# One plan for the order of every engine's work, and y of a block in two halves of its tokens: attention with two feed-forward layers on one core

## The chip, the cores and the metric

One core of one Trainium2 chip runs the kernel. The metric is the device time of an execution in microseconds (us). Names of engines: PE is TensorE (matmuls), DVE is VectorE, ACT is ScalarE, POOL is GpSimd, SP is SyncE, whose queue issues nearly all DMAs.

## What is computed

```python
def reference(q, k, v, moe_w_in, moe_w_out, moe2_w_in, moe2_w_out):
    scores = q @ k.T / sqrt(64)                   # 4 batches, 8 heads, 576 tokens, 64 wide
    scores = where(0 <= rel < 128, scores - slope[h] * abs(rel), -1e9)
    x = (softmax(scores) @ v)                     # 2304 tokens x 512
    h = x @ moe_w_in                              # 512 -> 2048
    x = where(h > 0, h, exp(min(h, 0)) - 1) @ moe_w_out      # ELU, 2048 -> 512
    h = x @ moe2_w_in
    return (h * sigmoid(h)) @ moe2_w_out          # SiLU
```

The four weights come as 64-bit numbers, and the kernel makes 32-bit ones of them on the chip.

## The kernel before

**Precision.** Every large product is made of three matmuls: each operand is split into an upper half (a copy by ACT to the matmul's number type) and a lower half (what is left, a subtraction on DVE), and upper x upper, upper x lower and lower x upper are summed in PSUM. So each operand costs ACT and DVE an instruction before PE can use it. Names end in `h` and `l` for the halves.

**Weights.** A piece of weights is loaded into one of four `wraw` tiles (`load_w`, four early ones into a part of `acc`), rescaled on POOL and ACT (`rescale`, L146 and L148), joined to 32 bits on DVE (`sign` L153, `join` L158) and split (`halves`, L166 and L167). Weights of the first matrix are taken in pairs: `first`, `second` and `third` in `parts` form the sums for the seven products below (L200 to L206). The early eight weights have their lower halves made on POOL.

**Attention** runs in 36 units (a pair of 128-token groups by a pair of heads). A unit's scores (L501), the masking and row minimum on DVE (L509), the exponential on ACT (L514), the division on POOL (L560), the turn of the scores on PE (L540) with copies on DVE (L548) and ACT (L550), and the product with the values (L579, one for two units) are recorded by a hand-written loop, one unit per pass. In its gaps (`point`, `pop`) stand pieces of layer 1 for the first four of its 2048/128 = 16 slices of width, block by block of 512 tokens: `hidden` (h, L326) and `output` (y, L362). The fifth block comes after attention, together with 16 pieces of the fourth that are held back (`RESERVE`).

**The other slices** run in 15 steps, called k0 to k14 here: layer 1 in two sweeps of six slices over three blocks of 768 tokens (k0 to k2, k3 to k5), layer 2 in sweeps of six, six and four slices (k6 to k8, k9 to k11, k12 to k14). In a step, each pair of slices is one `quad`: seven products (L901) of the weights' sums with seven sums of x (the operands, made by `make` on ACT and DVE, or reloaded by `reload` from DRAM; `make_far` makes those of k6 early and stores them through the tile `xo`) instead of eight. Copies of partial results (`snap`, tiles `hs` and `h`, ACT L908), sums (`add`, DVE L912) and activations (L860 to L881) follow each, and what they give is split in `gh` and `gl`. Then y: eight or six groups of matmuls (L998), each added to `acc` on DVE (L1012). The last two pieces of y (six matmuls each) are put between the first products of the next step (`pend`, L1110). The seven tiles of the second matrix's weights (`w1h`, `w1l`) come free when y of the last block of a sweep is done.

**What sets the order.** The program is written down engine by engine in the order of the calls. Behind each product or piece of y stands `between`, which has an allowance in us: it runs the next stage of the activation chains (`chain`), then operations from `urgent` (the operands) and from `weight_op` as far as the allowance lasts. During attention, `weight_step` does so in fixed units (`WSLOTS`). Each engine runs its own list strictly in this order. Tiles come from rings of buffers.

Of the kernel before, what the change touches and what calls it, by code (L numbers as in the profile page):

```python
# [26 lines left out]
class Ring:  # L27


    def __init__(self, pool, n):  # L30
        self.slots = [pool] * n

    def add(self, pool, n):
        self.slots = [pool] * n + self.slots

    def next(self):
        pool = self.slots.pop(0)
        self.slots.append(pool)
        return pool
# [3 lines left out]
def attention_elu_silu_kernel(  # L43
# [21 lines left out]
    NFF = DFF // P  # L65
    scale = 1.0 / float(D) ** 0.5
    blocks = [(0, 2)] + [(g, 4) for g in range(2, NG, 4)]
    FIRST = {b * S // P for b in range(B) if b * S % P == 0}
    MID = {b * S // P: b * S % P for b in range(B) if b * S % P}
    AFTER = {g + 1: r for g, r in MID.items()}  # L70

    NB = len(blocks)
# [6 lines left out]

# [3 lines left out]
    NPRE = 2  # L83
    PAIRS = 3
    OUTS = 7
    OPEN = 5
    LAG = 7
    RESERVE = 16
    ORDER = ((0, 1, 2), (2, 1, 0)), ((2, 1, 0), (0, 1, 2), (2, 1, 0))
    WSLOTS = [*range(15), *range(24, 36)]  # L90
    PIECES = (1, 1, 2)
    BANKS = 3
    UNITS = [(t, hp) for t in range(NG // 2) for hp in range(NPAIR)]
    home = {}
    for bi, (g0, n) in enumerate(blocks):
        for g in range(g0, g0 + n):
            home[g] = bi, (g - g0) * P

    left = lambda name, bufs, **kw: ctx.enter_context(tc.tile_pool(name=name, bufs=bufs, side="left", **kw))
    acc_p = left("acc", 1)  # L100
    wraw_p = left("wraw", NRAW)
    dram_p = ctx.enter_context(tc.tile_pool(name="dram", bufs=1, space=bass.MemoryType.DRAM))
    early = ExitStack()
    e_p = early.enter_context(tc.tile_pool(name="e0", bufs=1, side="right"))
    g_p = early.enter_context(tc.tile_pool(name="g0", bufs=FIRST_F, side="right"))
    w_p = early.enter_context(tc.tile_pool(name="w0", bufs=FIRST_F, side="right"))
    x_p = early.enter_context(tc.tile_pool(name="x0", bufs=1, side="right"))
    banks = Ring(ctx.enter_context(tc.tile_pool(name="ps_m", bufs=BANKS, space=PSUM)), BANKS)

    def bank(name):  # L110
        return banks.next().tile([P, 4 * P], F32, tag="m", name=name)
# [3 lines left out]
    xt = {}  # L115

    ws = [(w1_in, w1_out), (w2_in, w2_out)]
    weights = {}
    owed = []
    raws = {}  # L120

    def load_w(kind, layer, f):
        w = ws[layer][kind]
        i = tasks.index((kind, layer, f))
        if i in SCRATCH:

            bi, i = SCRATCH[i]
            t = acc[bi][:, i * 2 * NKC * P:(i + 1) * 2 * NKC * P]
            t = t.bitcast(U32).rearrange("p (f w) -> p f w", w=2)
        else:  # L130
            t = wraw_p.tile([P, NKC * P, 2], U32, tag="wraw", name="wraw")
        if kind == 0:
            nc.sync.dma_start(
                t.rearrange("p (c f) w -> p c (f w)", c=NKC),
                w[:, f * 2 * P:(f + 1) * 2 * P].rearrange("(c p) f -> p c f", p=P))
        else:
            nc.sync.dma_start(t.rearrange("p f w -> p (f w)"), w[f * P:(f + 1) * P, :])
        raws[kind, layer, f] = t

    def rescale(kind, layer, f):  # L140

        t = raws[kind, layer, f]
        low, top = t[:, :, 0], t[:, :, 1]


        nc.gpsimd.tensor_scalar(f32(top), f32(top), 2.0 ** -112, 1.0, op0=ALU.mult, op1=ALU.mult)  # L146

        nc.scalar.activation(low.bitcast(I32), low, AF.Copy, scale=7.49 * 2.0 ** -32)  # L148

    def sign(kind, layer, f):  # L150
        t = raws[kind, layer, f]
        low, top = t[:, :, 0], t[:, :, 1]
        nc.vector.scalar_tensor_tensor(low, top, 0x80000000, low, op0=ALU.bitwise_and, op1=ALU.bitwise_or)  # L153

    def join(kind, layer, f):
        t = raws[kind, layer, f]
        low, top = t[:, :, 0], t[:, :, 1]
        nc.vector.scalar_tensor_tensor(top, top, 3, low, op0=ALU.logical_shift_left, op1=ALU.bitwise_or)  # L158

    def halves(pool, tag, src, w):  # L160

        h = pool.tile([P, w], F32R, tag=f"{tag}h", name=f"{tag}h")
        lo = pool.tile([P, w], F32R, tag=f"{tag}l", name=f"{tag}l")

        def lower(eng=nc.vector):
            eng.tensor_tensor(lo, f32(src), f32(h), op=ALU.subtract)  # L166
        return (h, lo), lambda: nc.scalar.activation(h, f32(src), AF.Copy), lower  # L167

    def parts(kind, layer, f):

        full = NKC * P
        w = full // 2
        if kind == 1 or (layer == 0 and f < FIRST_F):
            top = raws.pop((kind, layer, f))[:, :, 1]
            early_one = layer == 0 and f < FIRST_F
            pair, upper, lower = halves(w_p if early_one else out_p[0], f"w{kind}", top, full)

            def done():
                lower(nc.gpsimd if early_one else nc.vector)
                weights[kind, layer, f] = pair  # L180
            return [(0.0, upper), (0.7, done)]
        if f % 2 == 0:
# [3 lines left out]
            def done():  # L186
                lower()
                weights[kind, layer, f] = pair
# [28 lines left out]
    def part(kind, layer, f):  # L217
        for _, fn in parts(kind, layer, f):
            fn()
# [934 lines left out]
```

## Time and profile before

| | |
|---|---|
| time, median of 3 runs | 962.9 us (961.23 to 963.43) |
| the profiled execution: time, span | 966.37 us, 964.6 us |
| PE busy | 888.9 us (92%) |
| DVE, ACT, POOL busy | 608.0, 500.1, 134.3 us |
| mean granted TensorE clock | 0.966 of full |

The span is the time from the first to the last instruction. An engine is busy while one of its instructions runs; time in which it waits is idle, and the trace names the instruction that ended the wait. PE is busy nearly all the time, so its idle time and its slow stretches are what can be read as loss.

### The profile page before, as it was taken

How to read it: one execution, taken by the hardware profiler on the slowest of the kernel's cores; microseconds unless marked ns; L12 is line 12 of the kernel's file. 1: busy time of each engine (PE TensorE's matmuls, PEld its weight loads, DVE VectorE, ACT ScalarE, POOL GpSimd, SP SyncE). 2: the span in 40 equal slices, each digit the busy share in tenths (PEclk: the TensorE clock that was granted, in tenths of full speed). 3: DMA queues.
4: the chain of work that ended last, by engine and by line, in shares of the span. 5: the costliest groups of instructions: out<-in, count | busy, mean ns of one | idle time of the engine just before them, and what ended most of it. 6: DMA issues, size and time to landing. Idle time of an engine off the chain costs nothing. (4 is left out here: it accounts for less than half of the span.)

```text
span 964.6 us, 15023 instructions
## 1 busy us (share of the span) xinstructions
PE 888.9 (92%) x5520; PEld 786.2 (82%) x5520; DVE 608.0 (63%) x1375; ACT 500.1 (52%) x1191; POOL 134.3 (14%) x248
## 2 busy tenths in 40 slices
PE   6788998988788999988999798999998999999998
PEld 4666775666688999988999797798888898889997
DVE  6866658647687877887666766664566442564343
ACT  6666676645473646465444546564656151534321
POOL 7753332321110000111000011000011000000000
PEclk9789999989899999999999899999999999999999
DMA  9224263314712610246072832515136332116541
GB/s 315 91 84 141 78 215 112 96 50 180 280 48 97 241 34 1 88 163 241 3 304 87 318 128 89 220 31 229 44 109 218 120 128 102 43 46 229 203 157 66
DMA packets 55929, 131.00 MB, mean 136 GB/s; under 512 B 3760, under 2 KB 35760, under 8 KB 55856
## 3 DMA queue, kind: packets, MB, share of 16 engines
q1 hardware_dynamic: 55712, 129.91, 37.7%
q8 instruction: 44, 0.72, 0.3%
q14 instruction: 29, 0.24, 0.1%
q10 hardware_dynamic: 144, 0.13, 0.0%
HBM read 93.06 MB, written 36.96 MB: 135 GB/s over the span
## 5 line engine op out<-in xcount | busy, mean ns | idle before, releaser
L881 DVE TENSOR_TENSOR gl<-e,gh 128x384 fp32r<-128x384 f32 x168 | 94.2, 565 | 81.0 <-ACT gh L861 76.0
L146 POOL TENSOR_SCALAR wraw<-wraw 128x512 f32<-128x512 f32 x60 | 44.1, 736 | 574.4 <-DMA wraw<-in_moe_w_in_dram 277.2
L998 PE MATMUL y<-w1l,gh 128*128 128x512 f32 (+1 forms) x292 | 113.6, 389 | 0.5 <-DVE w1l L166 0.5
L998 PE MATMUL y<-w1h,gh 128*128 128x512 f32 (+1 forms) x292 | 113.6, 389 | 0.4 <-ACT w1h L167 0.4
L998 PE MATMUL y<-w1h,gl 128*128 128x512 f32 (+1 forms) x292 | 113.6, 389 | 0.0
L998 PE MATMUL y<-gh,w1h 128*128 128x384 f32 x288 | 97.7, 339 | 4.7 <-ACT w1h L167 4.7
L998 PE MATMUL y<-gl,w1h 128*128 128x384 f32 x288 | 97.6, 339 | 0.8 <-DVE gl L881 0.8
L998 PE MATMUL y<-gh,w1l 128*128 128x384 f32 x288 | 97.8, 340 | 0.3
L1012 DVE TENSOR_TENSOR acc<-y,acc 128x384 f32<-128x384 f32 (+2 forms) x85 | 51.4, 607 | 72.4 <-PE y L998 72.4
L514 ACT ACTIVATE p<-p,neg 128x192 f32<-128x192 f32 (+1 forms) x144 | 62.9, 439 | 30.0 <-DVE neg L509 30.0
L560 POOL TENSOR_SCALAR p<-p,sm 128x192 f32<-128x192 f32 (+1 forms) x144 | 62.0, 449 | 107.0 <-DVE sm L518 86.2
L998 PEld LDWEIGHTS y<-w1h,gl 128*128 128x128 f32 x292 | 55.3, 189 | 11.3
L908 ACT ACTIVATE hs<-b 128x384 f32<-128x384 f32 x42 | 20.2, 481 | 85.3 <-PE b L901 85.3
L998 PEld LDWEIGHTS y<-w1h,gh 128*128 128x128 f32 x292 | 55.2, 189 | 10.4 <-ACT w1h L167 0.8
L998 PEld LDWEIGHTS y<-w1l,gh 128*128 128x128 f32 x292 | 55.2, 189 | 10.3 <-DVE w1l L166 0.8
L998 PEld LDWEIGHTS y<-gh,w1h 128*128 128x128 f32 x288 | 54.9, 190 | 5.4 <-ACT w1h L167 5.4
L998 PEld LDWEIGHTS y<-gh,w1l 128*128 128x128 f32 x288 | 54.9, 191 | 1.3 <-DVE w1l L166 1.3
L998 PEld LDWEIGHTS y<-gl,w1h 128*128 128x128 f32 x288 | 54.8, 190 | 1.2 <-DVE gl L881 1.2
L901 PE MATMUL b<-t,wbh 128*128 128x384 f32 x168 | 44.8, 347 | 11.6 <-DVE hs L912 11.6
L540 PEld LDWEIGHTS pt<-ident,p 64*128 64x128 f32 x544 | 23.8, 152 | 37.2 <-POOL p L560 27.3
L901 PE MATMUL b<-t,wch 128*128 128x384 f32 x168 | 45.3, 351 | 9.5 <-ACT hs L908 9.5
L877 ACT ACTIVATE gh<-e 128x384 fp32r<-128x384 f32 x72 | 36.8, 524 | 32.7 <-DVE e L312 18.7
(157 smaller groups left out, 2183.0 us busy)
## 6 DMA issues: line engine op xcount, KB each, us to landing
t<-d SPq DMA_DIRECT2D x28, 768.0 KB, 6.3
wraw<-in_moe_w_in_dram SPq DMA_DIRECT2D x32, 512.0 KB, 5.5
b<-d SPq DMA_DIRECT2D x21, 768.0 KB, 6.0
wraw<-in_moe_w_out_dram SPq DMA_DIRECT2D x28, 512.0 KB, 3.8
d<-t SPq DMA_DIRECT2D x16, 768.0 KB, 7.3
d<-b SPq DMA_DIRECT2D x12, 768.0 KB, 3.8
k<-in_k_dram SPq DMA_DIRECT2D x16, 384.0 KB, 5.5
d<-xo SPq DMA_DIRECT2D x7, 768.0 KB, 3.6
```

Of the source, the lines that this page charges most:

```text
L146: nc.gpsimd.tensor_scalar(f32(top), f32(top), 2.0 ** -112, 1.0, op0=ALU.mult, op1=ALU.mult)
L514: nc.scalar.activation(dst, dst, AF.Exp, bias=m, scale=-1.0, accum_out=a)
L540: nc.tensor.transpose(ps[:, x, j, i, :], pt[half, j, e, c - x * PAD:c - x * PAD + P], ident[half, half])
L560: nc.gpsimd.tensor_scalar(dst, dst, by, 1.0, op0=ALU.mult, op1=ALU.mult)
L877: nc.scalar.activation(gh[:, s], tiles["e"], AF.Copy)
L881: nc.vector.tensor_tensor(gl[:, s], tiles["e"], f32(gh[:, s]), op=ALU.subtract)
L901: nc.tensor.matmul(t[name][:, 0:HALF], a[:, cs], x[:, j, c, :], start=(start and c == 0 and n == 0), stop=(c == 1 and n == 2), skip_group_ ...
L908: nc.scalar.activation(t[name], t[src][:, 0:HALF], AF.Copy)
L998: nc.tensor.matmul(t["ps"][:, 0:w], l, r, start=(f == 0 and x == 0), stop=(f == n - 1 and x == 2))
L1012: nc.vector.tensor_tensor(dst, t["ps"][:, 0:w], dst, op=ALU.add)
```

## The change

The order of the calls no longer sets the order on the engines. Every operation is first added to a plan, with its engine, an assumed duration, what it reads and writes and, for PE, a due time; from these the latest useful start of every other operation follows, back along its users. Then a list scheduler plays the whole kernel: whenever an engine is free, it takes the ready operation with the earliest latest start and writes it down. `Ring`, `between`, `weight_op`, `weight_step`, `WSLOTS`, `point`, `pop`, `RESERVE` and the allowances are gone; tiles are fixed, with dependences by key.

```diff
+class Plan:
+    LINK = 0.2
+    DMA_START = 1.8
+    DMA_RATE = 220.0e3
...
+    def run(self):
+        for op in reversed(self.ops):
+            op.late = min([op.due] + [b.late - self.LINK - op.cost - op.tail for b in op.before])
...
+                for eng in queues:
+                    if eng and free.get(eng, 0.0) > now:
+                        continue
+                    can = [x for x in queues[eng] if max(x[0], x[1].floor) <= now]
...
+                    x = min(can, key=lambda x: (x[1].late, x[1].n))
...
+                    if op.moved:
+                        port = max(port, now + self.DMA_START) + op.moved / self.DMA_RATE
+                        end = port
```

An operation is added like this; the early lower halves of the weights, and the two `gl` of the last early block, go to DVE:

```diff
-            def done():
-                lower(nc.gpsimd if early_one else nc.vector)
+        if layer == 0 and f < FIRST_F:
+            tag = ("w0", kind, f)
+            split_weight(tag, None, top, None, 4 * P, top_k, "DVE")
...
-            eng = nc.gpsimd if bi == NB - 1 and f < 2 else nc.vector
-            eng.tensor_tensor(gl[:, 0:w], tiles["e"][:, 0:w], f32(gh[:, 0:w]), op=ALU.subtract)
+        add("DVE", 0.15 + w / 950.0, lambda: nc.vector.tensor_tensor(T[gk[1]][:, 0:w], T[ek][:, 0:w], f32(T[gk[0]][:, 0:w]),
+                                                                 op=ALU.subtract), r=[ek, gk[0]], w=[gk[1]])
```

The units of attention are due every 5.2 us, and the pieces of a block are due evenly from the time its x is expected to that of the next block's. Three tiles hold turned scores instead of two. The activations' tiles `e` are three instead of four. The tiles `gh` and `gl` now hold a half of a block's tokens; y is done by halves, and the second half is merged into the first nine products of the next step:

```diff
-            first, rest = pieces[:OPEN], pieces[OPEN:]
-            return ([p for g in first for p in g[:-1]] + [g[-1] for g in first] + [p for g in rest for p in g])
+        return [[g for h, g in groups if h == half] for half in range(2)]
...
+    def merge(a, b):
+        if not b:
+            return list(a)
+        out = []
+        for i, x in enumerate(a):
+            out.append(x)
+            lo, hi = i * len(b) // len(a), (i + 1) * len(b) // len(a)
+            out += b[lo:hi]
+        return out
...
-            pend = ys[-2:] if k + 1 < len(steps) else []
-            for fn in ys[:len(ys) - len(pend)]:
+            for fn in merge(order[:SPAN], owed) + order[SPAN:]:
                 fn()
-                between(1.04 if layer == 0 else 1.36)
...
+            first, second_half = outputs(k)
+            first = open_first(first)
+            second_half = [p for g in second_half for p in g]
+            first = first[:2] + over[:1] + first[2:3] + over[1:] + first[3:]
+            if k + 1 < len(steps) and SPAN:
+                owed = second_half
```

The number of instructions on PE, ACT and SP and of DMAs is the same. What stands where:

On POOL in the first units (L560 and L492 are the scaling of a unit's scores `p`; L166 is a weight's lower half; L146 and L315 rescale a weight), before:

```order
L483 COPY biasa<-bias 128x1536
L484 MEMSET biasa 64x8x64
L166 TENSOR_TENSOR w0l<-wraw,w0h 128x512
L146 TENSOR_SCALAR wraw<-wraw 128x512
L560 TENSOR_SCALAR p_120<-p_120,sm 128x128
L560 TENSOR_SCALAR p_120<-p_120,sm 128x192
L560 TENSOR_SCALAR p_120<-p_120,sm 128x128
L560 TENSOR_SCALAR p_120<-p_120,sm 128x192
L166 TENSOR_TENSOR w0l<-wraw,w0h 128x512
L146 TENSOR_SCALAR wraw<-wraw 128x512
```

and now:

```order
L436 MEMSET biasa 64x8x64
L492 TENSOR_SCALAR p_127<-p_127,sm_151 128x128
L492 TENSOR_SCALAR p_127<-p_127,sm_151 128x192
L492 TENSOR_SCALAR p_127<-p_127,sm_151 128x128
L492 TENSOR_SCALAR p_127<-p_127,sm_151 128x192
L315 TENSOR_SCALAR raw_85<-raw_85 128x512
L315 TENSOR_SCALAR raw_86<-raw_86 128x512
L492 TENSOR_SCALAR p_128<-p_128,sm_153 128x192 x4
```

The subtractions between the units' scalings have gone from POOL.

On PE where attention ends (`a` is the product with the values, `pt` and `t` the turn of the scores, L362 and L614 y of the fourth early block, L326 and L587 h of the fifth), before, where 48 matmuls of y follow in a row:

```order
L540 MATMUL pt<-ident,p_122 128x64 x16
L579 MATMUL a<-ptt,v_118 64x256 x2
L579 MATMUL a<-ptt,v_118 64x128 x2
L579 MATMUL a<-ptt,v_119 64x128 x2
L579 MATMUL a<-ptt,v_118 64x256 x2
L579 MATMUL a<-ptt,v_118 64x128 x2
L579 MATMUL a<-ptt,v_119 64x128 x2
L362 MATMUL y<-gh,w1h 128x512
L362 MATMUL y<-gl,w1h 128x512
L362 MATMUL y<-gh,w1l 128x512
```

and now, where the last 12 of y follow and mix with h:

```order
L543 MATMUL a<-pt_143,v_125 64x256 x2
L543 MATMUL a<-pt_143,v_125 64x128 x2
L543 MATMUL a<-pt_143,v_126 64x128 x2
L614 MATMUL m_157<-g_97,w_99 128x512
L614 MATMUL m_157<-g_100,w_99 128x512
L614 MATMUL m_157<-g_97,w_102 128x512
L614 MATMUL m_157<-g_103,w_105 128x512
L614 MATMUL m_157<-g_106,w_105 128x512
L614 MATMUL m_157<-g_103,w_108 128x512
L587 MATMUL m_156<-x_121,w_98 128x512
L587 MATMUL m_156<-x_122,w_98 128x512
L587 MATMUL m_156<-x_121,w_101 128x512
```

Most of the fourth block's y has moved ahead of the end of attention.

On DVE where k2 passes to k3 and a sweep changes (L912 and L886 are the sums `hs` of a quad, L1012 and L978 add a group of y to `acc`, L166 and L295 make the lower half of a new sweep's weight), before:

```order
L158 SCALAR_TENSOR_TENSOR wraw<-wraw 128x512
L166 TENSOR_TENSOR w1l<-wraw,w1h 128x512
L153 SCALAR_TENSOR_TENSOR wraw<-wraw 128x512
L1012 TENSOR_TENSOR acc_80<-y,acc_80 128x384
L881 TENSOR_TENSOR gl<-e,gh 128x384
L158 SCALAR_TENSOR_TENSOR wraw<-wraw 128x512
L912 TENSOR_TENSOR hs<-b,hs 128x384
L166 TENSOR_TENSOR w1l<-wraw,w1h 128x512
L311 TENSOR_SCALAR e<-e 128x384
L312 TENSOR_TENSOR e<-hs,e 128x384
L912 TENSOR_TENSOR hs<-a,hs 128x384
```

and now:

```order
L978 TENSOR_TENSOR acc_80<-m_2654,acc_80 128x384
L572 TENSOR_SCALAR e_2645<-e_2645 128x384
L573 TENSOR_TENSOR e_2645<-hs_2639,e_2645 128x384
L851 TENSOR_TENSOR g_2804<-e_2643,g_2803 128x384
L851 TENSOR_TENSOR g_2802<-e_2645,g_2801 128x384
L295 TENSOR_TENSOR w_2826<-raw_87,w_2825 128x512
L295 TENSOR_TENSOR w_2828<-raw_84,w_2827 128x512
L978 TENSOR_TENSOR acc_80<-m_2656,acc_80 128x384
L295 TENSOR_TENSOR w_2830<-raw_85,w_2829 128x512
L886 TENSOR_TENSOR h_2642<-m_2652,h_2642 128x384
L295 TENSOR_TENSOR w_2832<-raw_86,w_2831 128x512
L886 TENSOR_TENSOR hs_2641<-m_2653,hs_2641 128x384
```

Before, the new weights' lower halves stood one by one among their own preparation and the quad's sums; now four of them stand together at the end of the second half of y.

## Rows read from the trace of the kernel before

**Rows 1.** The page: busy us (share) of each engine; TensorE's clock in 40 slices.

```profile
PE 888.9 (92%) x5520; PEld 786.2 (82%) x5520; DVE 608.0 (63%) x1375; ACT 500.1 (52%) x1191; POOL 134.3 (14%) x248
...
PEclk9789999989899999999999899999999999999999
```

**Rows 2.** Windows, one for each stage: columns in the first row, clock behind.

```profile
core 0: us, PE busy (x) PEld busy (x) DVE busy (x) ACT busy (x) POOL busy (x), PEclk, DMA share, GB/s
0.00:62.10 62.10, 43.68 (x438) 30.78 (x438) 48.24 (x159) 40.27 (x132) 44.45 (x85) 0.84 0.51 168
62.10:213.10 151.00, 136.10 (x1436) 101.60 (x1435) 94.00 (x353) 100.48 (x308) 49.70 (x111) 0.95 0.36 114
213.10:256.80 43.70, 37.29 (x144) 28.62 (x145) 30.57 (x55) 20.39 (x43) 5.13 (x5) 0.88 0.65 238
256.80:313.60 56.80, 48.79 (x260) 46.05 (x259) 44.01 (x82) 32.61 (x68) 4.72 (x7) 0.97 0.27 91
313.60:408.90 95.30, 94.22 (x541) 93.90 (x541) 74.57 (x150) 51.38 (x108) 2.79 (x4) 1.00 0.25 91
408.90:567.10 158.20, 147.23 (x813) 143.67 (x812) 111.39 (x218) 78.98 (x162) 9.07 (x12) 0.97 0.48 180
567.10:865.50 298.40, 285.74 (x1406) 254.50 (x1405) 167.16 (x297) 144.66 (x305) 18.42 (x24) 0.99 0.32 117
865.50:961.40 95.90, 95.81 (x493) 87.05 (x491) 37.70 (x65) 31.34 (x69) 0.00 (x0) 1.00 0.44 163
```

**Rows 3.** Windows without a wait: k1, k7, a pair of units, y of L362.

```profile
313.60:360.60 47.00, 47.00 (x272) 47.00 (x272) 37.47 (x76) 25.79 (x55) 0.00 (x0) 1.00 0.37 139
...
623.30:669.70 46.40, 46.40 (x235) 42.13 (x234) 24.52 (x47) 25.33 (x55) 0.65 (x1) 1.00 0.36 139
...
117.27:127.54 10.27, 10.27 (x113) 7.83 (x113) 5.28 (x24) 7.66 (x24) 3.32 (x9) 1.00 0.56 162
...
213.10:223.90 10.80, 10.80 (x47) 8.91 (x48) 1.00 0.50 170
```

**Rows 4.** Waits of PE: total us, times, longest.

```profile
PE pt L540 <- ACT ptt L550: 19.2, 14, 3.4
PE b L901 <- DVE hs L912: 11.6, 13, 2.9
PE b L901 <- ACT hs L908: 9.5, 8, 5.4
PE y L998 <- ACT w1h L167: 5.1, 3, 2.7
```

**Rows 5.** Timeline of DVE at 419 us and of ACT at 535 us.

```profile
418.98 0.54 DVE L912 TENSOR_TENSOR hs<-b,hs 128x384 f32<-128x384 f32 x1
420.68 0.69 DVE L166 TENSOR_TENSOR w1l<-wraw,w1h 128x512 fp32r<-128x512 f32 x1 [1.16 <-ACT w1h L167]
...
534.80 0.94 ACT L801 ACTIVATE xo<-acc 128x384 fp32r<-128x384 f32 x2 [3.94 <-DMA d<-xo]
```

**Rows 6.** Timeline of POOL and PE at 22 to 25 us.

```profile
22.63 1.29 POOL L166 TENSOR_TENSOR w0l<-wraw,w0h 128x512 fp32r<-128x512 f32 x1
...
24.51 0.78 POOL L560 TENSOR_SCALAR p<-p,sm 128x128 f32<-128x128 f32 x1
...
25.35 0.88 PE L540 MATMUL pt<-ident,p 64*128 64x64 f32 x6 [3.56 <-POOL p L560]
```

**Rows 7.** Groups by line: busy us, mean ns of one, idle before.

```profile
L166 POOL TENSOR_TENSOR w0l<-wraw,w0h 128x512 fp32r<-128x512 f32 x4 | 5.6, 1406 | 1.8 <-ACT w0h L167 1.8
L345 POOL TENSOR_TENSOR gl<-e,gh 128x512 fp32r<-128x512 f32 x2 | 2.6, 1316 | 31.9 <-ACT gh L339 31.9
...
L166 DVE TENSOR_TENSOR w1l<-wraw,w1h 128x512 fp32r<-128x512 f32 x28 | 20.0, 724 | 22.2 <-ACT w1h L167 22.2
L345 DVE TENSOR_TENSOR gl<-e,gh 128x512 fp32r<-128x512 f32 (+1 forms) x18 | 11.7, 648 | 6.9 <-ACT gh L339 6.4
```

**Rows 8.** Timeline of DVE: the second operands of k0.

```profile
235.10 1.01 DVE L731 TENSOR_TENSOR b<-xs,b 128x384 fp32r<-128x384 f32 x2
```

**Rows 9.** DMA issues: reloads of operands, KB each, median us to landing.

```profile
t<-d SPq DMA_DIRECT2D x28, 768.0 KB, 6.3
```

More of the change, by code (lines that the diff above doesn't have):

```diff
@@ L24, in f32, with __init__ @@
     return ap.bitcast(F32)
[L27 to L39, printed above, removed]
+class Op:
+    def __init__(self, eng, cost, fn, due, tail, n):
+        self.eng, self.cost, self.fn, self.due, self.tail, self.n = eng, cost, fn, due, tail, n
+        self.after, self.before = set(), set()
+        self.start = self.end = None
@@ new lines, in reload, with source @@
+    def reload(k, i):
+        layer, sw, b = steps[k]
+        load(lambda: nc.sync.dma_start(f32(T["c", i].rearrange("p x c t -> p (x c t)")), scratch[layer, b, i]), 768 * 1024,
+             r=[("d", layer, b, i)], w=c_keys(i))
+    def source(k):
+        layer, sw, b = steps[k]
+        if k and steps[k - 1][::2] == (layer, b):
+            return "same"
+        if k == FAR:
+            return "load"
+        return "make" if not any(s[::2] == (layer, b) for s in steps[:k]) else "load"
+    ns = {"hs": 0, "h2": 0, "e": 0, "g0": 0, "g1": 0, "below": 0}
@@ new lines, in m7, with m4, m3, outputs @@
+        def m7():
+            product(6, "b", False)
+            sum_of("s5", "b")
+            active("s5", 1, 1)
+        def m4():
+            product(3, "b", False)
+            active("b", 1, 0)
+        def m3():
+            product(2, "c", False)
+            sum_of("s2", "c")
+            active("s2", 0, 1)
+        return [m1, m2, m6, m5, m7], [m4, m3]
+    def outputs(k):
+        layer, sw, b = steps[k]
+        f0, f1 = SWEEPS[layer][sw]
+        n = f1 - f0
+        groups = []
+        size = 2 * NKC if layer == 0 else BIG // P
+        for j in range(size):
+            half = j // (size // 2)
+            parts = 2 if k == len(steps) - 1 and j == size - 1 else 1
+            for part in range(parts):
+                st = {}
@@ L1069, in layers @@
-        made_y = [output(NB - 1, c) for c in range(NKC)]
-        for c, f in together(range(NKC), range(FIRST_F), 3):
-            pieces, after = made_y[c]
-            pieces.pop(0)()
-            if not pieces:
-                for r in after:
-                    r()
-            between(0.68)
-        flush(urgent)
-        early.close()
-        late["g"] = ctx.enter_context(tc.tile_pool(name="g1", bufs=MOST_F, side="right"))
-        out_p.append(ctx.enter_context(tc.tile_pool(name="w1", bufs=OUTS, side="right")))
```

1515 lines of the change are left out of this document (718 added, 797 removed).

## The prediction

> **What bounds the kernel now.** I read the engines' busy shares first. TensorE (PE) is busy 888.9 us of 964.6, against 608.0 for VectorE (DVE) and 500.1 for ScalarE (ACT) [rows 1]: PE is the bound, and only its lost time can be won. The busy share hides part of that loss, because a matmul at half clock counts as busy too. So I then cut the span into stages [rows 2] and set each against a stretch without a wait [rows 3]: a layer-1 block of the feed-forward part (three groups of seven products, then y) takes 47.0 us with PE busy throughout, a layer-2 block of 6 slices 46.4 us, and two attention units with their share of the feed-forward part (24 matmuls) 10.27 us.
>
> The loss by stage: the first twelve units take 62.1 us with PE busy 43.68 at a granted clock of 0.84; there the loaded engines are DVE (48.24) and GpSimd (POOL, 44.45). Units 13 to 36 take 151.0 us against 12 x 10.27 = 123.2. The 144 matmuls behind the last attention product take 43.7 us; at 10.80/47 = 0.23 us each [rows 3] they need 33.1, so 10.6 are lost. The first layer-1 block k0 takes 56.8 against 47.0 less two y pieces that fall into the next block (12 matmuls at 47.0/272 = 0.17 us, 2.1), so 11.9 are lost; k1 and k2 lose 95.3 - 94.0 = 1.3; k3 to k5 158.2 - 141.0 = 17.2; six layer-2 blocks 298.4 - 278.4 = 20.0. The last three lose nothing (PE 95.81 of 95.9).
>
> The waits of PE tell what is late: the copy of turned scores, a sum `hs` or a copy `hs` in a seven-product group, an upper half of a weight [rows 4]. No DMA stands there. DVE and ACT run their queues in order, and work that PE waits for stands behind work that waits for something else: at 418.98 DVE makes the sum `hs`, and the next group's sums stand behind a `w1l` that waits 1.16 us for ACT; at 534.80 ACT has waited 3.94 us for a store to free `xo`, and the copy `hs` that PE needs stands behind it [rows 5]. In the first units PE waits 3.56 us at 25.35 for POOL's scaling, which at 24.51 stands behind a weight subtraction of 1.29 us [rows 6].
>
> **The change, part by part.** The arithmetic and the transfers are the same in number; the change is order, tiles and ten subtractions.
>
> *Ten subtractions from POOL to DVE.* Eight early weight halves cost POOL 1.3 to 1.4 us each, two `gl` 1.316; on DVE the weight shape takes 0.724, a `gl` 0.648 [rows 7]. DVE gains 8 x 0.724 + 2 x 0.648 = 7.1 us, POOL loses about 8 x 1.35 + 2.6 = 13.4. Who waits behind them on DVE are the masked scores and copies of the units. In the first stage DVE then has 48.24 + 5.8 = 54.0 us of work, the lower bound of that stage; the upper is 62.1 + 5.8 = 68, if each subtraction delays a unit. The case nearest to it is the wait at 25.35 that goes away, so I take 58.
>
> A page of the Trainium skill speaks against this part: "SBUF — State Buffer", section "SBUF: two separate sides", says that a VectorE instruction with two SBUF inputs and a GpSimd instruction that reads SBUF exclude each other for the whole instruction. By it the eight subtractions would now hold up POOL's scalings for another 5.8 us; the trace bears the rule out only loosely.
>
> *Units 13 to 36.* 123.2 us, plus 5 for two turns and two value products of earlier units that fall into the stage (an estimate: a pair less 24 x 0.23 = 5.5 leaves 4.8 for two scores, two turns and one value product), plus 36 of the 48 y matmuls that before stood behind the last attention product and now stand among the units: 36 x 0.23 = 8.3. Floor 136.5. The loss is 22.5 now and lies between that and nothing; the order gives PE ready work wherever a unit is late, so I take 6. Last attention product at 58 + 136.5 + 6 = 200.5 (now 213.1).
>
> *From there to block k1.* PE has 12 + 96 matmuls at 0.23 = 24.8 us and k0's 44.9, together 69.7. DVE has what it did in these two stages, 30.57 + 44.01 = 74.6 us, plus the two `gl`: 76. So DVE becomes the bound here, and the saving is smaller than PE's loss. The highest DVE share that goes with a full PE in the rows is 37.47 of 47.0, 80%; at that share 76 us take 95, at 100% 76. I take 83 (now 100.5). The other cover, the operands of k0, is not late: before they were being made 23 us behind the last attention product (235.10 against 213.1 [rows 8]), and PE has 25 us of work until then.
>
> *y in halves.* The second half of a block's y now stands among the next block's products, twelve pieces (six matmuls each) among nine products, where before two pieces in all did. That hides the chain product, copy, sum, activation, halves. It also frees the next sweep's tiles of `w1` later: with seven tiles and six in use, five must wait until y of the last block of a sweep has ended, now (12 + 9) x 6 x 0.17 = 21 us into the next block instead of 5. The order has those five `w1` subtractions on DVE directly behind the last sums of that y. k1 and k2: 94 + 2 = 96, the 2 for the denser DVE (bounds 94 and 102, the latter if DVE needs 80% for 74.57 + 7). k3 to k5: 141 + 3 = 144 (141 to 158.2). Six layer-2 blocks: 278.4 + 4.6 = 283 (278.4 to 298.4); the remainders are a fifth of today's loss, since DVE is busy only 111.39 of 158.2 and 167.16 of 298.4 there and has room for everything if it stands in the right order. Last three: 95.9. Tail 964.6 - 961.4 = 3.2.
>
> *Queues.* The reloads of operands and the weight loads share SP's queue, before and after; the cover is that PE never waited for a DMA [rows 4].
>
> Sum: 200.5 + 83 + 96 + 144 + 283 + 95.9 + 3.2 = 905.6 us of span. The profiled execution took 966.37 at a span of 964.6, so +1.8; it was 3.5 above the median of 962.9, so -3.5. **904 us.**
>
> **The rivals.** *1. The loss at the changes of sweep stays.* The late release of `w1` puts all of a sweep's weight work into the same few us; only attention, k0 and the chain waits gain. For it: both stages with a large loss hold such changes, k3 to k5 one and the six layer-2 blocks two, while k1 and k2 without one lose 1.3. Against it: the 3.94 us behind `xo` [rows 5] and its like are not of that kind. If three quarters of 37.2 + 1.3 stay (29) rather than the 9.6 of my sum, and DVE sets the stage before (90 instead of 83): 904 + 19 + 7 = 930.
>
> *2. The floor is nearly reached.* First stage 54, units 138.5, the stage at DVE's bound 78, then 95, 142, 280, 95.9, 3.2: 886.6 - 1.7 = 885. For it: when PE has no holes its clock is granted in full (1.00 in the whole rows of [rows 3], 0.84 and 0.88 in the two holed stages of [rows 2]), so each closed hole pays twice. The Trainium skill, "TensorE: Matmul & The Clock Gate", Part 1, says the same as a rule: the throttled clock is the default and activity releases it. Against it: DVE at 97% in the transition.
>
> *3. Slower than before.* SP's queue is one line. A reload of an operand waits on SP until the last product that reads the old operand; a weight load behind it waits too, and now the issue order rests on assumed landing times. If at each of the 14 block changes PE waited for one landing of 6.3 us [rows 9], that is 88: 992. It decides from 59/14 = 4.2 us a change. Against it: no DMA in PE's waits, and half of the block changes have no reload.
>
> *4. The new order moves nothing that matters*, since DVE's work per block is what sets the time: within 0.2% of 962.9. Against it: DVE has 607.6 + 7.1 us, far below 904.
>
> **How the numbers follow.** Forecast (about 892 to 918) 0.58, floor 0.15, loss at sweeps 0.20, slower 0.05, nothing 0.02. The likeliest is the forecast: 904. To leave out no more than 2 in 10 the range takes in the floor's centre and most of rival 1, with its unknown costs: 884 to 938. A measurement of this kernel can tell about 0.2% from no change. Faster 0.58 + 0.15 + 0.20 = 0.93, within 0.2% 0.02, slower 0.05.
>
> **What would show it.** Right: the last attention product near 200 us with little feed-forward work left behind it; DVE above 85% busy between there and k1; layer-1 blocks from k1 on at 47 to 48 us; the `hs` waits nearly gone from PE's list; granted clock near 1.00 from k1 on. Wrong: PE waiting for `w` halves in the third group of k3 or of the first layer-2 block (rival 1), or a DMA as releaser of PE, ACT or DVE at block changes (rival 3); a first stage above 62 us would say that the subtractions on DVE cost more than POOL gave back.

## The result, and the profile after

The changed kernel takes **893.4 us** (median of 4 runs, 892.67 to 894.52) against 963.2 for the kernel before beside it: ratio 0.928 (0.9262 to 0.9298), 69.8 us less. The forecast was 904 with a range of 884 to 938: right in direction and inside the range, 10.6 us too high. The profiled execution took 892.67 us, its span is 890.9 us.

In the listing, `scores` is now L454, the turn L511, the value product L543, the early feed-forward products L587 and L614, the seven products L873, y L964. From the page of the profile after, the lines that answer to [rows 1]:

```profile
PE 867.2 (97%) x5520; PEld 774.6 (87%) x5520; DVE 600.8 (67%) x1385; ACT 503.1 (56%) x1191; POOL 132.0 (15%) x238
...
PEclk9979999999979999999999999999999999999999
```

The windows of after, cut at the same events as [rows 2] (unit 11's scores, the last value product, k1, k3, k6, k12; the third row holds both stages between the last value product and k1):

```profile
core 0: us, PE busy (x) PEld busy (x) DVE busy (x) ACT busy (x) POOL busy (x), PEclk, DMA share, GB/s
0.00:53.00 53.00, 39.12 (x454) 27.43 (x454) 42.43 (x160) 40.76 (x130) 39.69 (x80) 0.95 0.79 266
53.00:194.70 141.70, 141.45 (x1456) 102.94 (x1455) 101.14 (x369) 100.79 (x314) 49.83 (x108) 0.98 0.30 95
...
194.67:269.21 74.54, 68.97 (x333) 62.16 (x332) 63.95 (x120) 51.87 (x105) 8.75 (x10) 0.93 0.59 205
...
269.20:359.40 90.20, 90.20 (x518) 90.20 (x518) 76.58 (x157) 53.68 (x112) 2.91 (x4) 1.00 0.28 100
359.40:501.00 141.60, 141.60 (x812) 141.60 (x811) 108.09 (x210) 74.51 (x154) 9.90 (x12) 1.00 0.46 173
501.00:782.00 281.00, 280.33 (x1423) 255.26 (x1422) 168.57 (x305) 149.14 (x309) 20.93 (x24) 1.00 0.37 138
782.00:887.70 105.70, 105.59 (x535) 95.04 (x533) 39.70 (x68) 32.40 (x69) 0.00 (x0) 1.00 0.42 148
```

In the second row and from the fourth on PE is busy as long as the row lasts. What is left to lose stands in the first 53 us, 13.9 us idle, and in the third row, 5.6 us idle and a clock of 0.93. PE's waits (total us, times, longest) show the same against [rows 4]: the chain waits of 12 and 19 us are gone.

```profile
PE s L454 <- DVE bias L421: 3.7, 1, 3.7
PE t L511 <- POOL p L492: 3.2, 5, 1.0
PE s L454 <- DVE neg L465: 3.1, 3, 1.3
PE t L511 <- ACT pt L523: 2.9, 2, 2.6
PE m L964 <- DVE h L886: 2.8, 1, 2.8
PE m L964 <- DVE g L851: 1.2, 1, 1.2
```

### The profile page after: what moved, and what is told of

Its sections match the earlier page's. It is cut to its first block, busy times and chain, and to the rows that moved or that the text cites. A ratio compares the mean times of both kernels' runs of the same rounds, so it can differ in the third digit from the quotient of the medians.

```text
span 890.9 us, 14913 instructions
## 1 busy us (share of the span) xinstructions
PE 867.2 (97%) x5520; PEld 774.6 (87%) x5520; DVE 600.8 (67%) x1385; ACT 503.1 (56%) x1191; POOL 132.0 (15%) x238
## 4 chain that ended last, share of the span: by engine, by line
PE 89%; DVE 7%; ACT 2%; POOL 1%; issue 1%; POOLq 0%; DVEq 0%; ACTq 0%
PE m L964 38%; PE m L873 34%; PE m L614 5%; PE m L587 5%; PE a L543 3%; PE s L454 3%; PE t L511 2%; DVE c L734 1%; DVE raw L318 1%; DVE w L295 1%; DVE p L465 1%; DVE raw L320 1%; DVE t L759 0%; DVE e L572 0%; DVE e L573 0%
## 5 line engine op out<-in xcount | busy, mean ns | idle before, releaser
L964 PE MATMUL m<-w,g 128*128 128x512 f32 (+1 forms) x876 | 211.7, 387 | 0.0
L964 PEld LDWEIGHTS m<-w,g 128*128 128x128 f32 x876 | 161.6, 188 | 26.4
L964 PE MATMUL m<-g,w 128*128 128x384 f32 x864 | 165.4, 342 | 4.7 <-DVE h L886 2.8
L964 PEld LDWEIGHTS m<-g,w 128*128 128x128 f32 x864 | 154.9, 192 | 6.3 <-DVE h L886 3.1
L315 POOL TENSOR_SCALAR raw<-raw 128x512 f32<-128x512 f32 x60 | 50.8, 847 | 544.5 <-DMA raw<-in_moe_w_in_dram 233.3
L851 DVE TENSOR_TENSOR g<-e,g 128x384 fp32r<-128x384 f32 x168 | 92.6, 559 | 41.1 <-ACT e L837 39.4
L873 PE MATMUL m<-c,wd 128*128 128x384 f32 x504 | 101.4, 336 | 0.1
L873 PE MATMUL m<-c,wc 128*128 128x384 f32 x504 | 100.8, 336 | 0.0
L873 PE MATMUL m<-c,wa 128*128 128x384 f32 x504 | 99.5, 336 | 1.1 <-DVE c L734 0.6
L886 DVE TENSOR_TENSOR hs<-m,hs 128x384 f32<-128x384 f32 x84 | 46.7, 556 | 76.2 <-PE m L873 75.6
L978 DVE TENSOR_TENSOR acc<-m,acc 128x384 f32<-128x384 f32 (+2 forms) x85 | 51.4, 608 | 67.4 <-PE m L964 66.3
L873 PEld LDWEIGHTS m<-c,wa 128*128 128x128 f32 x504 | 89.1, 188 | 4.5 <-DVE acc L978 0.9
L873 PEld LDWEIGHTS m<-c,wd 128*128 128x128 f32 x504 | 89.0, 188 | 2.6 <-ACT h L882 0.4
L873 PEld LDWEIGHTS m<-c,wc 128*128 128x128 f32 x504 | 89.2, 188 | 2.2 <-DVE c L734 0.2
L492 POOL TENSOR_SCALAR p<-p,sm 128x192 f32<-128x192 f32 (+1 forms) x144 | 67.0, 484 | 97.2 <-DVE sm L486 58.7
L614 PE MATMUL m<-g,w 128*128 128x512 f32 (+1 forms) x240 | 60.1, 393 | 1.3 <-DVE ex L573 1.0
L587 PE MATMUL m<-x,w 128*128 128x512 f32 (+1 forms) x240 | 58.0, 382 | 0.0
L614 PEld LDWEIGHTS m<-g,w 128*128 128x128 f32 x240 | 42.5, 198 | 13.1 <-issue 2.7
L873 PE MATMUL m<-c,wb 128*128 128x384 f32 x252 | 50.6, 336 | 0.0
```

The costliest lines, as they stand in the source:

```text
L315: add("POOL", 0.75, lambda: nc.gpsimd.tensor_scalar(f32(top()), f32(top()), 2.0 ** -112, 1.0, op0=ALU.mult, op1=ALU.mult), w=top_k)
L492: nc.gpsimd.tensor_scalar(dst, dst, T["sm", u % 5][:, e, j:j + 1], 1.0, op0=ALU.mult, op1=ALU.mult)
L587: nc.tensor.matmul(T[m][:, 0:w], a[:, cs], T["x0", b2][:, c, 0:w], start=(c == 0 and x == 0), stop=(c == NKC - 1 and x == 2))
L614: nc.tensor.matmul(T[m][:, 0:w], a[:, cs], b2[:, 0:w], start=(f == 0 and x == 0), stop=(f == FIRST_F - 1 and x == 2))
L851: add("DVE", 0.58, lambda: nc.vector.tensor_tensor(T[gk[1]], T[ek], f32(T[gk[0]]), op=ALU.subtract), r=[ek, gk[0]], w=[gk[1]])
L873: nc.tensor.matmul(T[m][:, 0:HALF], a[:, cs], x[:, j, c, :], start=(begin and c == 0 and n == 0), stop=(c == 1 and n == 2), skip_group_che ...
```

## The experiments

The theory after the result: the gain comes from engines that no longer stand behind work that isn't ready; the half of y that is carried into the next block is a small help; the ten subtractions matter in the first stage. The rivals: the carried half brings the gain; the priority brings it; the subtractions bring it. "k0 starts" means its first product. An engine passes over an operation that isn't ready while the plan is made, by the plan's assumed durations; the list that comes of it is then run strictly in its order, in every kernel here.

### The carried half

**e1: no carry at all.**

```diff
-    SPAN = 9
+    SPAN = 0
```

> The changed kernel with the carrying of y's second half switched off: every block's y is finished before the next block's products. Theory A (the gain came from ready-first lists, and the carried half is a small part): between block starts TensorE is nearly saturated either way, since y's first half (12.5 us of matmuls in a block of layer 1) covers the last activation chain of the block; the time stays at 890 to 898 us, block periods 47.2 and 46.5 us as now. Theory B (the carried half is what fills the block changes): each of the 14 changes opens a wait again, 1.5 to 2 us apiece, and the time rises to 913 to 921 us.

Measured: **882.4 us**, ratio 0.9158 (0.9143 to 0.9172). Both theories missed: without the carry the kernel is 11 us *faster*. The rows to compare are PE's timeline in y of k0, first of after, then of this run (start, us, idle before and what ended it):

```profile
246.54 6.41 PE L964 MATMUL m<-g,w 128*128 128x384 f32 x36
255.72 2.08 PE L964 MATMUL m<-g,w 128*128 128x384 f32 x6 [2.77 <-DVE h L886]
258.46 0.69 PE L964 MATMUL m<-g,w 128*128 128x384 f32 x1 [0.66 <-ACT g L850]
260.30 9.07 PE L964 MATMUL m<-g,w 128*128 128x384 f32 x35 [1.16 <-DVE g L851]
```

```profile
248.26 22.01 PE L964 MATMUL m<-g,w 128*128 128x384 f32 x126
270.10 0.86 PE L873 MATMUL m<-c,wa 128*128 128x384 f32 x4
```

In after, the last stretch of y before k1 runs from 246.54 to 269.21, 22.7 us for 78 matmuls that need 13.5: it waits for the last sums and activations. Without the carry 126 matmuls stand there and run through in 21.84: their second half is the work that covers the wait. The change carries 72 matmuls of k0's y; 24 of them came forward in the list, and the other 48 stand at their places among k1's products.

**e5: no carry at k0 alone.**

```diff
-            if k + 1 < len(steps) and SPAN:
+            if 0 < k < len(steps) - 1 and SPAN:
```

> The changed kernel with the carrying of y's second half switched off at the first block (k0) alone; it stays at the other 13 changes. Theory A (the carry costs only where k0's y stands without work: its first half has 13.5 us of matmuls and took 22.7 us, while the second half, 8.3 us more, is held back among the products of k1): k0's y of 126 matmuls runs through in about 21.9 us and the time is 881.5 to 885 us, as without any carry, which is 882.4. Theory B (the carry costs something at every change): 888 to 893 us.

Measured: **886.4 us** (ratio 0.9212, 0.9187 to 0.9237), between the two. About 7 of the 11 us belong to k0, and about 4 to the other changes, which Theory A had at nothing. Windows over one block, k3 and k10, of after and then of e1 show a part of the 4:

```profile
359.37:406.56 47.19, 47.19 (x271) 47.19 (x271) 40.48 (x75) 25.96 (x52) 6.64 (x8) 1.00 0.55 206
689.05:735.53 46.48, 46.48 (x236) 42.15 (x234) 18.21 (x33) 15.27 (x33) 0.00 (x0) 1.00 0.32 120
```

```profile
365.22:412.14 46.92, 46.92 (x272) 46.92 (x272) 39.86 (x77) 23.82 (x50) 6.17 (x6) 1.00 0.48 174
691.87:738.23 46.36, 46.36 (x235) 42.12 (x234) 15.38 (x27) 15.05 (x33) 0.00 (x0) 1.00 0.33 120
```

The same matmuls (a record more or less is missing), PE busy throughout, and 0.27 and 0.12 us more with the carry. That makes 1.3 us over the three blocks of layer 1 and the four of layer 2 that are whole in e5 (k3 to k5, k8 to k11). Another 2 us stand in k6 and k7, where layer 1 passes to layer 2: e5, and below it e9, which has the same matmuls there in the lump (e9 is described next):

```profile
494.71:589.79 95.08, 94.37 (x487) 86.67 (x487) 71.10 (x136) 59.15 (x124) 9.28 (x8) 1.00 0.50 188
```

```profile
493.76:586.80 93.04, 93.04 (x487) 86.67 (x487) 74.64 (x140) 59.70 (x126) 10.23 (x11) 1.00 0.48 181
```

PE stops there for 0.7 us with the spread carry and not at all in e9; the other 1.3 us are not taken apart.

**e9: no carry at k0, and elsewhere in one lump instead of spread.**

```diff
-    SPAN = 9
+    SPAN = 1
```

> No carry at k0, and from k1 on the carried pieces stand in one lump behind the next block's first product, instead of being spread among nine; to be compared with 886.4 us (spread) and 882.4 us (no carry). In the spread version each run of six matmuls that ends in a change between products and y takes 1.06 us where 1.04 is the matmuls' own time, 0.02 us a change, and a block of layer 1 takes 47.19 us against 46.91 without the carry. Theory A (the carry's cost after k0 is this price of changes): the lump has few changes, block periods go to 46.9 to 47.0 and 46.4 us, and the time is 882 to 884 us. Theory B (it is late release: banks, or tiles of w1 and g held into the next block): the periods stay, or waits come at the block's start, and the time is 886 us or more.

In layer 1 a sum of products is begun in this kernel in a PSUM bank that still holds another, so its values are not the reference's; the instructions, their shapes and their number are. Measured: **882.8 us** (0.916, 0.9145 to 0.9175), Theory A. Its windows for two such blocks, k4 and k10:

```profile
399.84:446.80 46.96, 46.96 (x271) 46.96 (x271) 34.70 (x72) 20.96 (x45) 0.00 (x0) 1.00 0.43 168
679.55:725.93 46.38, 46.38 (x235) 42.13 (x234) 15.37 (x27) 15.05 (x33) 0.00 (x0) 1.00 0.32 120
```

In such a block PE goes from products to y or back 21 times with the spread carry, 5 times without and 7 times with the lump (layer 2: 23, 5, 7). 0.27/16 = 0.017 us a change in layer 1, 0.12/18 = 0.007 in layer 2. Late release of banks or tiles would show as waits, and in these blocks PE has none.

**e10: the kernel before without its own carry of two pieces.**

```diff
-            pend = ys[-2:] if k + 1 < len(steps) else []
+            pend = []
```

> The kernel before with its own carry switched off: it keeps the last two pieces of y back and sets them between the next block's first products; here each block's y is finished first. Orders otherwise as before. Theory A (an order fixed ahead needs the carry, since the next block's first operations are not ready at its start): 14 changes lose 1 us or more apiece, 975 to 990 us. Theory B (the carry covers nothing there either): 958 to 966 us.

Measured: **973.1 us** against 963.8, ratio 1.0115 (1.0083 to 1.0147). On Theory A's side, a little under its range, but not 1 us at each of 14 changes: in the profiled executions the whole difference (971.4 and 964.6 us of span) stands in k5, 57.8 us for 54.8, and k6, 60.6 for 56.2. PE's longest wait in this run, whose row answers to [rows 4]:

```profile
PE b L901 <- ACT hs L908: 13.2, 8, 9.3
```

The longest wait for a copy `hs` has grown from 5.4 to 9.3 us. In an order fixed ahead the carried pieces cover a copy that comes late; in the list the pieces carried out of k0 were moved away from where they were needed.

### The order

**e4: ready operations by their number in the program.**

```diff
-                    x = min(can, key=lambda x: (x[1].late, x[1].n))
+                    x = min(can, key=lambda x: x[1].n)
```

> The changed kernel with the list's choice among ready operations made by their number in the program instead of by lateness. Theory A (what matters is that an engine never stands behind an operation that is not ready; which ready one it takes matters little): 890 to 905 us, block periods within 1 us of 47.2 and 46.5. Theory B (the lateness rule carries the gain): the weights' preparation and the next block's combinations fall behind, waits of several us at block changes, over 915 us.

Measured: **918.5 us** (0.9532, 0.9508 to 0.9555), Theory B by the number, but not for its reason. Windows of this run, then of after, cut at the last value product and at k0:

```profile
0.00:219.77 219.77, 183.88 (x1923) 136.55 (x1923) 147.95 (x528) 144.84 (x445) 95.65 (x188) 0.99 0.39 126
219.77:249.12 29.35, 24.59 (x95) 19.51 (x94) 24.48 (x43) 18.81 (x37) 2.80 (x4) 0.88 0.49 173
249.12:918.40 669.28, 660.42 (x3505) 623.25 (x3503) 433.87 (x815) 338.04 (x710) 33.59 (x46) 0.99 0.40 147
```

```profile
0.00:194.67 194.67, 180.54 (x1909) 130.35 (x1909) 143.57 (x528) 141.56 (x443) 89.51 (x188) 0.97 0.44 142
194.67:220.22 25.55, 25.18 (x111) 20.30 (x110) 19.51 (x36) 17.15 (x33) 1.81 (x2) 1.00 0.47 158
220.22:890.90 670.68, 661.50 (x3505) 623.94 (x3503) 437.73 (x823) 344.43 (x716) 40.68 (x48) 0.99 0.41 148
```

From k0 on, with the carry in both, the priority is worth nothing (669.3 and 670.7 us). All of the 27.5 us between the two profiled executions arise before it: in the attention, where units, weights and feed-forward work compete for the same engines, taking the operation due first brings the last value product 25 us forward. The largest part is in the first units: unit 11 starts at 70.9 instead of 53.0, and PE's longest wait is there, for POOL, which also rescales the early weights:

```profile
30.75 0.37 PE L511 MATMUL t<-ident,p 64*128 64x64 f32 x2 [14.20 <-POOL acc L315]
```

**e8: lateness, but in a fixed order; no carry.** VectorE, ScalarE and GpSimd may only take the unissued operation with the earliest latest start.

```diff
+        rows = {}
+        for op in sorted(self.ops, key=lambda op: (op.late, op.n)):
+            rows.setdefault(op.eng, []).append(op)
...
+                    if eng in ("DVE", "ACT", "POOL"):
+                        can = [x for x in can if x[1] is rows[eng][0]]
```

> No carry, and VectorE, ScalarE and GpSimd take their operations strictly by lateness: each stands at the one due first until that one is ready, instead of taking the ready one due first. TensorE and the transfers go on as before. It is to be compared with 882.4 us. Theory A (not standing behind an operation that is not ready is what carries the gain): the engines stand often and TensorE waits for them at many block changes and in the attention, over 920 us. Theory B (a good priority is enough; an order fixed by it is as good as the list): within 10 us, 882 to 892 us.

Measured: **953.4 us** (0.9908, 0.9882 to 0.9934), Theory A: 71 us above 882.4, nearly the time of the kernel before. Its PE waits (its lines are six higher: products L879) and its longest DVE wait:

```profile
PE m L879 <- ACT h L888: 8.4, 11, 1.4
PE m L879 <- DVE e L850: 8.3, 2, 4.5
PE m L879 <- DVE acc L984: 8.1, 5, 3.8
...
DVE hs L892 <- PE m L879: 93.8, 29, 13.7
```

DVE now stands up to 13.7 us before one operation with others ready behind it (6.5 in after); it costs time where PE runs dry by it. k0 takes 68.3 us for 48.2, k3 57.9 for 46.9. So the same plan is worth 81 us (963 to 882) when an engine may pass over what is not ready, and 9 (962 to 953) when it may not. The windows of e8 from unit 11 to the last value product, of k3 to k5 and of k6 to k11 show where it costs:

```profile
63.51:203.99 140.48, 139.33 (x1454) 103.21 (x1454) 86.10 (x340) 93.75 (x302) 46.76 (x109) 0.99 0.28 89
393.80:548.67 154.87, 145.15 (x812) 141.29 (x811) 105.71 (x210) 77.04 (x159) 9.84 (x11) 0.99 0.48 175
548.67:847.78 299.11, 287.48 (x1405) 256.62 (x1406) 162.78 (x303) 144.97 (x307) 20.39 (x25) 0.98 0.33 121
```

Behind k0 these are nearly the times of before (158.2 and 298.4 [rows 2]; e1: 140.7 and 278.6). Between unit 11 and the last value product they are not: there e8 in its fixed order loses nothing against e1 (141.5 us), so in that stage a fixed order by lateness is as good as the list.

### The subtractions

**e2: the eight early lower halves back on GpSimd.**

```diff
-            split_weight(tag, None, top, None, 4 * P, top_k, "DVE")
+            split_weight(tag, None, top, None, 4 * P, top_k, "POOL")
```

> The changed kernel with the eight early lower halves w0l back on GpSimd, all else left to the scheduler. Theory A (GpSimd bounds the first stage): it is busy 34 of the first 44 us now, and eight times about 1.4 us puts 11 us more on it, so that unit 11 starts 3 to 9 us later than 53.0 us and the time is 896 to 902 us. Theory B (the list puts them where GpSimd has time, after the rush): 892 to 894.5 us, unit 11 within 1 us of 53.

Measured: **893.8 us** (0.9275, 0.9261 to 0.929), the changed kernel's time, as Theory B has it, but the place speaks for A: unit 11 starts at 56.0 instead of 53.0, the last value product ends 1.6 us later, and k0 starts at 221.97 instead of 220.22. In k0's y the delay is gone again: k1 starts at 269.16 (after: 269.21). Not by shorter waits, which are 2.31 + 1.17 + 1.16 = 4.6 us there as in after, but behind them: the last 35 matmuls of that stretch take 7.76 us for 9.07 in after (row in e1), at a granted clock of 0.84 over the stretch for 0.77. Whether that is luck or comes of the order, no run tells.

**e3: the kernel before with the ten subtractions on VectorE.**

```diff
-                lower(nc.gpsimd if early_one else nc.vector)
+                lower(nc.vector)
...
-            eng = nc.gpsimd if bi == NB - 1 and f < 2 else nc.vector
+            eng = nc.vector
```

> The kernel before with only the eight early lower halves, and the two gl of the last block, moved from GpSimd to VectorE; orders and y as before. Theory A (GpSimd's order alone held the first stage): TensorE's 3.6 us wait at 25 us goes, and the time falls by 2 to 5 us, to 958 to 961 us. Theory B (the move pays only with a list that places them): VectorE's fixed order puts the subtractions ahead of the units' own work, and the time is 962 us or more. Either way the move alone cannot carry more than a tenth of the 70 us.

Measured: **962.6 us**, ratio 0.9992 (0.9981 to 1.0003): no difference, as Theory B has it.

**e12: the subtractions on GpSimd where nothing later hides it** (on the kernel of e11 below).

> The kernel of the run with measured costs (no carry, 300 GB/s, five costs; 878.9 us) with the eight early lower halves on GpSimd at an assumed cost of 1.45 us. There TensorE waits twice for VectorE's elu, 2.3 us each, between 50 and 56 us, while VectorE is busy 14.7 of 15 us from 40 to 55 and GpSimd 6.1. Theory A (VectorE is the bound from 40 to 55, and eight times 0.72 us off it shortens that stretch): 875 to 878 us. Theory B (GpSimd's 11 us come in the first 40 us, where it is busy 33 of 40 and the units wait for its scaled p): 879 to 883 us.

Measured: **883.2 us** (0.9181, 0.9165 to 0.9197) against 878.9: 4.3 us slower, Theory B by the number, but the place is not the first 40 us alone: the eight stand between 23 and 64 us, and GpSimd's busy time grows most from 40 to 55 us (10.9 us for 6.1). Unit 11 starts 1.4 us later than in e11, the last value product ends 4.8 us later, at 199.3.

So the move to VectorE is worth about 4 us in the kernel of e11; in the change as made it brought nothing measurable, since the 1.7 us that k0 starts earlier are lost again before k1.

### What the list assumes

**e6: 300 GB/s for 220, carry and all; e7: the same without the carry.**

```diff
-    DMA_RATE = 220.0e3
+    DMA_RATE = 300.0e3
```

> The changed kernel, carry and all, with one number of the scheduler changed: it assumes 300 GB/s for the transfers instead of 220 (the trace shows 327 GB/s between 220 and 246 us). Theory A (the wait in k0's y comes from an order made for weights that land later than they do: the combinations of k1 stand ahead of the sums h and of the weights of y on VectorE): the wait of 9 us falls under 3 us, and the time is 884 to 888 us. Theory B (VectorE is full there, 8.7 of 9 us busy from 255 to 264, and no order helps): 891 to 894.5 us.

> The changed kernel without the carry and with 300 GB/s assumed. Theory A (without the carry k0's y has no wait, so a better order there gives nothing; what is left is the first stage's 53 us): 880 to 883 us, as with 220. Theory B (an order made for earlier landings also brings the weights and the units of the first stage forward): 875 to 880 us.

Measured: **888.2 us** (0.9229, 0.9211 to 0.9247) and **881.2 us** (0.9158, 0.9133 to 0.9184). e6 comes out at the edge of Theory A (884 to 888): one number in the plan takes 5 us. DVE's timeline of after shows what the wrong number had done: the operands `c` of k1 stand ahead of the last sums `h` of k0, although PE needs `h` first.

```profile
252.30 1.96 DVE L734 TENSOR_TENSOR c<-xs,c 128x384 fp32r<-128x384 f32 x4
254.18 0.55 DVE L886 TENSOR_TENSOR h<-m,h 128x384 f32<-128x384 f32 x1
254.64 0.55 DVE L734 TENSOR_TENSOR c<-t,c 128x384 fp32r<-128x384 f32 x1
255.11 0.55 DVE L886 TENSOR_TENSOR h<-m,h 128x384 f32<-128x384 f32 x1
```

In e6 the wait for `h` is gone; what is late next is an upper half of a weight:

```profile
252.07 0.62 PE L964 MATMUL m<-g,w 128*128 128x384 f32 x2 [1.77 <-ACT w L292]
```

Without the carry (e7 against e1) the number makes 1.2 us, within the spread of the runs: k0 runs without a wait (46.9 us for 48.2), but unit 11 starts at 58.2 (e1: 54.7), in a profiled execution 2.6 us over e7's median.

**e11: e7 with five assumed durations put nearer to the traced ones.**

```diff
-                add("POOL", 0.45, scaled, r=sm, w=[("p", u % 3, j, e)])
+                add("POOL", 0.56, scaled, r=sm, w=[("p", u % 3, j, e)])
```

and likewise 0.75 to 0.85, 0.40 to 0.45, 0.70 to 0.75 and 0.60 to 0.67.

> No carry, 300 GB/s assumed, and five costs that the scheduler assumes for the attention put nearer to the durations in the trace (GpSimd's scaling of p 0.56 us for 0.45, its scaling of raw weights 0.85 for 0.75, VectorE's bias step 0.45 for 0.40 and its copy out of t 0.75 for 0.70, ScalarE's exponential 0.67 for 0.60). To be compared with 882.4 us (no carry) and 881.2 us (no carry, 300). Theory A (the waits left in the first 62 us come from an order made for wrong durations): unit 11 starts 1 to 4 us earlier and the time is 877 to 880 us. Theory B (that stage is bound by the sum of the work of three engines, and the order is as good as any): 880.5 to 883 us.

Measured: **878.9 us** (0.9122, 0.9106 to 0.9138), the fastest of all, 14.5 us under the change as made. In Theory A's range. Unit 11 starts at 55.2, which is 2.9 us earlier than in e7, as Theory A said, but no earlier than in e1 (54.7). The last value product ends 2.0 us earlier than in e1, and k0 runs without a wait, as in e7:

```profile
219.77:266.66 46.89, 46.89 (x271) 46.85 (x271) 44.71 (x86) 32.97 (x69) 6.22 (x8) 1.00 0.64 230
```

DVE is busy 44.7 of 46.9 us there, so a nearly full DVE does go with a full PE.

## Why the prediction came out 10 us high

| stage | predicted | measured |
|---|---|---|
| to unit 11's scores | 58 | 53.0 |
| to the last value product | 142.5 | 141.6 |
| to k1 | 83 | 74.5 |
| k1, k2 | 96 | 90.2 |
| k3 to k5 | 144 | 141.6 |
| k6 to k11 | 283 | 281.1 |
| k12 to k14 | 95.9 | 105.6 |
| tail | 3.2 | 3.3 |
| span | 905.6 | 890.9 |

**The reading of what bounds the kernel** held: PE's lost time was all there was to win, and the waits for `hs`, turned scores and weight halves went [rows 4, 5]. **The cause** held for most of it: with DVE, ACT and POOL standing behind work that isn't ready (e8), 71 of the 81 us between before and e1 come back, from k3 on nearly in the same stages as before. That before's own loss arose in this way is read from [rows 4, 5, 6]; no run shows it directly. For the units from 11 on it does not hold: there e8 loses nothing.

**The first stage** was mis-sized, 58 for 53.0. It was taken from between a floor of 54 and 68, as the price of subtractions on DVE. But DVE had only 42.4 us of work before unit 11, less than before: the list puts weight work that is not due yet behind it. So the 54 was no floor.

**The second stage** is near by two errors that cancel. The prediction counts twelve units before 62.1 us. With 16 score matmuls a unit, the windows of the scores alone show eleven, in before and in after:

```profile
0.00:62.05 62.05, 15.88 (x176) 8.94 (x176) 0.83 0.51 168
```

```profile
0.00:53.00 53.00, 13.31 (x176) 7.46 (x176) 0.95 0.79 266
```

So 25 units remained, and the floor was 12.5 x 10.27 + 5 + 8.3 = 141.7, not 136.5. Measured 141.6: no loss at all, where I had taken 6. Before, the loss was by the same correction 151.0 - 133.4 = 17.6, not 22.5 (by the prediction's own terms 151.0 - 128.2 = 22.8).

**The stage to k1** fails in its reason, and with it most of the size. I had put DVE's 76 us of work there as the bound. DVE did 63.95 us in 74.5, since the list spread the rest, and e1 does the stage in 73.7 us with 48 more matmuls of PE (8.3 us). Nor was the floor 69.7: I let two pieces of k0's y go into k1 and not its half. With 48 matmuls carried the floor is 24.8 + 47.0 - 8.3 = 63.5, so 11.0 us are lost, near my 13.3, but to the carry at k0 and to the order of `h` (e1, e5, e6), not to DVE's load. What I named as cover ("that hides the chain") was the step that cost: I weighed only where the carried pieces arrive, not the place that they leave.

**From k1 on** the sum is right, 618.9 for 618.4, and again by two errors: the remainders of 2, 3 and 4.6 did not come in full, and the 8.3 us carried out of k0 did. The carry also shifts 4 us out of k1 and k2 (48 matmuls in, 72 out) and 9.6 into the last three. What it should take can be read from e1, which carries nothing: from k1 to the end 610.9 us, with the 8.3 carried in 619.2. After takes 621.7, tail included: 2.5 more, for the spread carry (e5).

**The rivals.** Rival 1, late tiles of `w1`: the windows from k3 to k11 show PE busy but for 0.7 us, and no weight is among its waits. It fell. Rival 2, the floor nearly reached, came nearest (886.6 of span for 890.9), though its stages differ from the measured ones by up to 10 us; e11, at 876.8, lies below it. Rival 3, SP's queue: no DMA releases PE at a block change. Rival 4, no change, fell with the time itself.

**The Trainium skill's rule on the shared port** ("SBUF — State Buffer", section "SBUF: two separate sides") has a VectorE instruction with two SBUF inputs and a GpSimd instruction that reads SBUF shut each other out for the whole instruction. By it, as the prediction estimates, the eight subtractions would hold GpSimd's scalings up for 5.8 us. The 144 scalings in before, in after and in e2, where the eight are on GpSimd again:

```profile
L560 POOL TENSOR_SCALAR p<-p,sm 128x192 f32<-128x192 f32 (+1 forms) x144 | 62.0, 449 | 107.0 <-DVE sm L518 86.2 <-PE s L501 7.1 <-PE a L579 6.6
```

```profile
L492 POOL TENSOR_SCALAR p<-p,sm 128x192 f32<-128x192 f32 (+1 forms) x144 | 67.0, 484 | 97.2 <-DVE sm L486 58.7 <-PE t L511 14.1 <-ACT ex L596 6.9
```

```profile
L492 POOL TENSOR_SCALAR p<-p,sm 128x192 f32<-128x192 f32 (+1 forms) x144 | 66.0, 476 | 86.4 <-DVE sm L486 51.3 <-PE t L511 8.0 <-DVE neg L465 5.9
```

They did get 5.0 us longer, but 4.0 of it comes with the new order and 1.0 goes with the eight. The rule itself shows in the trace: in after five of the eight subtractions run beside a scaling, which then takes 0.88 to 1.37 us instead of 0.42 (the mean of those beside no VectorE instruction), as this one of 0.69 us, beside which the second of two scalings takes 0.97:

```profile
34.45 0.69 DVE L295 TENSOR_TENSOR w<-raw,w 128x512 fp32r<-128x512 f32 x1 [0.18 <-ACT w L292]
```

```profile
33.95 1.49 POOL L492 TENSOR_SCALAR p<-p,sm 128x192 f32<-128x192 f32 x2
```

In e2 other VectorE instructions run beside the scalings instead, so the sums differ little. By e12 the move is a gain.

**What stays open.** Which of DVE's stands in e8 costs which microseconds was not taken apart. What brought the 17.6 us between unit 11 and the last value product is open: no run takes back the third tile of turned scores, whose copies were PE's longest wait in sum before (19.2 us [rows 4]), or the y pieces among the units; e4 shows only that by number instead of lateness the stage takes 148.7 us. The 3.5 us of e11 over e1 are 1.2 with the rate and 2.3 with the durations, neither well clear of the spread.

## What to carry to other kernels

Let each engine's order come from a list that skips what is not ready; here that was worth 71 us, most of it in k0 and at the changes of sweep, and the priority 25, all of it where two kinds of work compete. Then take away devices that were made to fill gaps in a fixed order, such as pieces carried into the next block: they now only forbid the list to use them where the gap is. And give the list the durations and rates of the trace: six numbers made 3.5 us without the carry, and one of them 5 with it.

## What the runs showed of the hardware

- PE pays for going from one group of matmuls to another and back: 0.017 us a change in layer 1 and 0.007 in layer 2 (e1, e5, e9), though it counts as busy throughout. In k3 of after the matmuls from the third to the seventh behind a change start 176 to 181 ns after one another in the mean, the others 172 to 174. Why the two layers differ, no run here shows.
- PE's clock at the hole in k0: in after, three waits of 4.6 us together between 252 and 261 bring the granted clock to 0.55 between 255 and 264 us (row below), most of it at the lower level of 1.2 GHz; with the hole filled (e1) it stays at 1.00. So the hole cost about twice its waits, 9.2 us; in e2 the same 4.6 us of waits cost 7.4. The Trainium skill, "TensorE: Matmul & The Clock Gate", Part 1, has it as a rule that the throttled clock is the default and activity releases it; here the trace agrees, 0.55 behind the waits and 1.00 without them.

```profile
255.00:264.00 9.00, 6.47 (x19) 5.56 (x20) 8.69 (x17) 7.00 (x14) 0.49 (x1) 0.55 0.55 167
```
